# The rare-case test at the end of an attention and mixture-of-experts kernel: where its register is loaded, and where the code it skips lies

## The chip, the cores and the metric

The kernel runs on one core of a Trainium2 chip. The metric is the device time of one execution in microseconds, taken as the median of several runs. Five runs of the kernel before gave a median of 460.94 us, between 460.52 and 461.74. One further execution was taken by the hardware profiler; it took 460.28 us.

## What is computed

Two parts follow each other. The first is multi-query attention: 8 batches of 384 positions, 16 query heads of 64 elements, one key and value head per batch. The second sends each of the 3072 tokens (1024 elements) to one of 16 experts, chosen in two steps, and weighs the expert's answer:

```python
scores = scale * np.matmul(q, k.transpose(0, 1, 3, 2))
attn = np.exp(scores - max) / (sum + 1e-09)
x = np.matmul(attn, v)            # heads side by side: (3072, 1024)
g_idx = argmax(x @ w_group)       # one of 4 groups
e_idx = argmax(xg @ w_expert[g])  # one of 4 experts of the group
h = np.maximum(xg[mask_e] @ w1[g, e], 0.0)
out[tok_idx] = (g_w * e_w)[:, None] * (h @ w2[g, e])
```

## The kernel before, in words

The kernel is built for the case that nearly all tokens of a batch choose the same expert. It runs, for each batch, only the expert that most of its tokens chose, over all 384 tokens of the batch ("first units"). The pairs of batch and expert that this leaves out are counted by flags (`extra`). One such pair, the **leftover**, is picked out with `early_pair` and computed on the main path, for at most 32 tokens. Any more pairs, or scores too large for an exponential without its maximum taken off, are the **rare case**: a block behind `tc.If(rare > 0)` at L809, with loops over the remaining pairs and, inside it, a slow form of the whole computation. With the inputs of this case the block is not entered.

Everything ahead of the block is unrolled, and its order is written out by hand (`tc.manual_schedule()` at L74): each engine runs its instructions in the order in which the source issues them. `fill(n)` puts the next n units of expert work (8 `h_unit`s and 6 `y_unit`s for each batch, L402 and L410) at that place of the order, so that TensorE (PE) has work while small steps wait.

The end of the order is what matters here. Behind the last batch's attention, the flags of the leftover are made (L707: `small`, the number of pairs not covered; L709: `nex`, the same as an integer, on VectorE, DVE). The leftover's tokens are turned (L715, L717), gathered (L723, L725) and sent through its two products: L732 with the Relu at L734 on ScalarE (ACT), a transpose (L738, copied by DVE at L740), and the last product at L746, which ACT scales into `yc` at L748. At L750 GpSimd (POOL) scatters `yc` into the output with an indirect DMA. Between these steps stand single `fill(1)`s. The very last, at L751, is a `y_unit` in two halves: `spread` (L458) first adds the leftover's rows that fall into the last 128 tokens (PE at L463, DVE at L465, ACT at L468, SyncE's (SP) store at L466), then DVE joins each half with `yl` at L454, and SP stores it at L445.

Behind that, from L753 to L758, DVE makes `raref` and `rarei` from `small` and from `okf` (the test of the scores, made at L526), and `nc.values_load` at L758 brings `rarei` into a register on all five engines, with one TENSOR_LOAD on each. L809 is the test of that register. In the built program it is a compare-and-branch on each engine. Which side of it lies next in the code is set by `preferred_fallthrough_block`:

- before, with `False`, the untaken side comes first: a short block on each engine that takes back semaphores (2 semaphore instructions on PE, DVE and ACT each, 9 on SP, 6 instructions on POOL) and ends in a jump over the whole rare block to the kernel's end. The rare block is 836 instructions long in the built program on PE, 212 on DVE, 200 on SP, 145 on POOL and 138 on ACT (PE's fp32 matrix products count once here);
- the kernel's end is the drain and the two barriers over all engines that the profile puts at L901. SP first waits there for the last count of every semaphore (12 instructions), and POOL gathers the five engines.

Of the kernel before, what the change touches and what calls it, by code (L numbers as in the profile page):

```python
# [9 lines left out]
FP32 = mybir.dt.float32  # L10
BF16 = mybir.dt.bfloat16
I32 = mybir.dt.int32
# [3 lines left out]
OP = mybir.AluOpType  # L16
AX = mybir.AxisListType.X
ET = mybir.EngineType
# [3 lines left out]
def kernel(  # L22
# [11 lines left out]
    nc = tc.nc  # L34
# [36 lines left out]
    pool = fast.enter_context(tc.tile_pool(name="work", bufs=2))  # L71
# [4 lines left out]
    def side(shape, dtype, name):  # L76
        return ps_s.tile(shape, dtype, tag="s", name=name)
# [351 lines left out]
    def first_units(b):  # L429
        rows = {}  # L430

        def place(st, cs):
            if cs.start == 0:
                rows[st] = pool.tile([P, Dm], FP32, tag="y", bufs=3, name="y")
            return rows[st][:, cs]

        def closes(st):
            return b == B - 1 and st == ST - 1

        def store(st, cs, y):  # L440
            if closes(st):
                if cs.start == 0:
                    leftover["row"] = y
                else:
                    nc.sync.dma_start(out=outv[b, :, st, cs], in_=y)  # L445
            elif cs.stop == Dm:
                nc.sync.dma_start(out=outv[b, :, st, :], in_=rows[st][:])

        def merge(st, cs, ps, y):
            if not closes(st) or cs.start == 0:  # L450
                return False
            if cs.start == CW:
                spread()
            nc.vector.scalar_tensor_tensor(out=y, in0=ps[:], scalar=gsel[b][:, st:st + 1], in1=leftover["y"][:, cs.start - CW:cs.stop - CW], op0=OP.mult, op1=OP.add)  # L454
            return True
        return moe_units(wts[b][0], wts[b][1], xbf[b], lambda: gsel[b], place, store, merge, lambda st, nh: 2 if closes(st) and nh == 1 else 1)
# [26 lines left out]
    def fill(n):  # L483
        while n > 0:
            if not units:
                if begun[0] >= B or begun[0] not in wts:
                    return
                units.extend(first_units(begun[0]))
                begun[0] += 1
            units.pop(0)()  # L490
            n -= 1
            ran[0] += 1
            if ran[0] == (FO + 2 * ST) * (B - 2) + FO:
                leftover_w1()
            if ran[0] == (FO + 2 * ST) * (B - 1):
                leftover_w2()
# [11 lines left out]
    bound = {}  # L508
# [65 lines left out]
    def leftover_w1():  # L574
        leftover["e"], leftover["b"] = parts_of(leftover["reg"])
        w1 = wpool.tile([P, KO, F], BF16, tag="w1", name="w1")
        load_w1(w1, leftover["e"])
        leftover["w1"] = w1

    def leftover_w2():  # L580
        w2 = wpool.tile([P, FO, Dm], BF16, tag="w2", name="w2")
        nc.gpsimd.dma_start(out=w2[:], in_=w2f[bass.ds(leftover["e"], 1)].rearrange("a p k f -> (a p) k f"))
        leftover["w2"] = w2
# [95 lines left out]
    small = pool.tile([P, 2], FP32, tag="small", bufs=1, name="small")  # L679
# [27 lines left out]
    nc.vector.tensor_sub(out=small[:, 1:2], in0=nfl[:], in1=small[:, 0:1])  # L707
    nex = pool.tile([1, 1], I32, tag="nex", bufs=1, name="nex")
    nc.vector.tensor_copy(out=nex[:], in_=small[0:1, 1:2])  # L709
    fill(3)  # L710
    xtok = []
    for st in range(ST):
# [26 lines left out]
    hc = pool.tile([P, 2, P], BF16, tag="qT", bufs=3, name="hc")  # L739
    nc.vector.tensor_copy(out=hc[:], in_=phT[:])  # L740
    fill(1)
    py = side([P, QW], FP32, "py")
    for g in range(4):
        for h in range(2):
# [2 lines left out]
    yc = pool.tile([P, QW], FP32, tag="pt", bufs=9, name="yc")  # L747
    nc.scalar.activation(out=yc[:], in_=py[:], func=ACTF.Copy, scale=gc[:, 0:1])  # L748
    leftover["yc"] = yc
    nc.gpsimd.indirect_dma_start(out=out4[0:4 * (N - P)], out_offset=bass.IndirectOffsetOnAxis(ap=rows[:], axis=0), in_=yc[:], in_offset=None, bounds_check=4 * (N - P) - 1, oob_is_err=False)  # L750
    fill(1)  # L751
    assert ran[0] == UNITS * B
    raref = pool.tile([1, 2], FP32, tag="raref", bufs=1, name="raref")  # L753
    nc.vector.tensor_scalar(out=raref[:, 0:1], in0=small[0:1, 1:2], scalar1=0.0, scalar2=None, op0=OP.is_gt)
    nc.vector.tensor_scalar(out=raref[:, 1:2], in0=bound["okf"][:], scalar1=-1.0, scalar2=1.0, op0=OP.mult, op1=OP.add)
    rarei = pool.tile([1, 1], I32, tag="rarei", bufs=1, name="rarei")
    nc.vector.tensor_add(out=rarei[:], in0=raref[:, 0:1], in1=raref[:, 1:2])
    rare = nc.values_load(rarei[0:1, 0:1], min_val=0, max_val=2, skip_runtime_bounds_check_because="a sum of two comparisons")  # L758

    def load_pair(pair):  # L760
        e_reg, b_reg = parts_of(pair)
# [44 lines left out]
        for u in pair_units(*load_pair(pair)):  # L806
            u()

    rare_block = tc.If(rare > 0, preferred_fallthrough_block=False)  # L809
    with rare_block:  # L810
      ids = list_rest()
      n_extra = nc.values_load(nex[0:1, 0:1], min_val=0, max_val=NPAIR, skip_runtime_bounds_check_because="a sum of 128 flags")
# [93 lines left out]
```

## Time and profile before

| | us |
|---|---|
| median of the 5 runs | 460.94 |
| the profiled execution | 460.28 |
| its span, first to last instruction | 458.8 |
| PE busy | 448.7 |
| DVE busy | 308.4 |
| ACT busy | 242.0 |
| POOL busy | 60.5 |

The profiled execution's own time holds 1.5 us that lie outside its span. All durations below come from that execution, and times of day count from the span's start. In the profile, an engine's name with a q behind it (SPq, PEldq) stands for its sequencer: register loads, branches, semaphore instructions and the issue of DMAs, which are not counted as busy time. PE's sequencer goes under PEldq, since PEld is its weight load. A line such as "L758 SPq TENSOR_LOAD x1: 551/551/551, 453.4 to 453.4" gives the shortest, median and longest duration in ns, and the first and the last start in us. Instructions themselves are fetched by DMA: the page lists 35 pieces (0.57 MB) on queue 8 and 19 (0.16 MB) on queue 14 for the whole span.

### The profile page before, as it was taken

Reading aid. Unit: us, or ns where it says so; the run is one execution under the profiler, and the core shown is the slowest. Engines: PE = TensorE matmul, PEld = TensorE weight load, DVE = VectorE, ACT = ScalarE, POOL = GpSimd, SP = SyncE. Lnnn points to the kernel's source line nnn. Section 1 sums busy time; section 2 is a strip of 40 time slices with the busy share of each in tenths; the row PEclk is TensorE's granted clock in tenths of the full one; section 3 lists DMA queues with packets and bytes.
Section 4 is the critical chain, followed back from the end, with each engine's and each line's share of the span. In section 5 each row is a group of like instructions: output and inputs, shape, how many; then the busy total and the mean of one; then the engine's idle time right before and its main releaser. Section 6 shows DMA issues by size and latency. Waiting matters only on the chain.

```text
span 458.8 us, 10188 instructions
## 1 busy us (share of the span) xinstructions
PE 448.7 (98%) x4196; PEld 199.8 (44%) x4208; DVE 308.4 (67%) x488; ACT 242.0 (53%) x345; POOL 60.5 (13%) x83
## 2 busy tenths in 40 slices
PE   8999999999999999999999999999999999999994
PEld 6333445333643345433553335433364334434552
DVE  4899965499717996099843997269970999573421
ACT  2966643676337753566346663376635764541331
POOL 1004003000120113000030000300130000500000
PEclk9999999999999999999999999999999999999998
DMA  8787997996699395992979848994859910799992
GB/s 161 92 147 113 216 215 112 259 201 138 108 181 255 71 196 88 233 228 72 156 110 261 152 108 134 160 258 89 170 97 231 235 59 28 110 210 233 277 230 105
DMA packets 152454, 74.55 MB, mean 162 GB/s; under 512 B 120256, under 2 KB 138944, under 8 KB 152400
## 3 DMA queue, kind: packets, MB, share of 16 engines
q0 software_dynamic: 28416, 37.81, 48.3%
q1 hardware_dynamic: 122656, 35.68, 33.4%
q8 instruction: 35, 0.57, 0.5%
q10 hardware_dynamic: 1328, 0.33, 0.3%
q14 instruction: 19, 0.16, 0.1%
HBM read 92.62 MB, written 19.01 MB: 243 GB/s over the span
## 4 chain that ended last, share of the span: by engine, by line
PE 89%; DMA 4%; issue 3%; DVE 1%; POOL 0%; ACT 0%; ACTq 0%; SPq 0%; POOLq 0%
PE s L251 28%; PE o L290 25%; PE hps L407 17%; PE yps L417 16%; PE gps L312 2%; DMA x_bf<-xbf 2%; DMA xe<-x_bf 2%; DMA qn<-in_q_dram 1%; PE qps L228 1%; POOL xbf L301 0%; DVE presum L261 0%; PE sm L273 0%; PE pb L715 0%; DVE rinv L280 0%; DVE xT L300 0%
## 5 line engine op out<-in xcount | busy, mean ns | idle before, releaser
L253 ACT ACTIVATE pt<-s 128x1024 f32<-128x1024 f32 x144 | 142.1, 1026 | 72.2 <-PE s L251 71.5
L251 PE MATMUL s<-qT,kT 64*64 64x512 f32 x1152 | 142.7, 594 | 0.0
L290 PE MATMUL o<-pt,v 64*64 64x512 f32 x1152 | 141.1, 590 | 0.0
L261 DVE TENSOR_TENSOR presum<-presum,pt 128x1024 f32<-128x1024 f32 x96 | 116.6, 1215 | 15.2 <-ACT pt L253 9.8
L407 PE MATMUL hps<-xbf,w 128*128 128x384 bf16 x512 | 86.7, 326 | 0.0
L417 PE MATMUL yps<-w,hT 128*128 128x512 bf16 (+1 forms) x380 | 85.0, 375 | 0.6
L259 DVE TENSOR_TENSOR presum<-pt 128x1024 f32<-128x1024 f32 x24 | 29.4, 1224 | 76.8 <-ACT pt L253 75.4
L290 PEld LDWEIGHTS o<-pt,v 64*64 64x64 f32 x1152 | 43.4, 133 | 76.8 <-issue 73.0
L251 PEld LDWEIGHTS s<-qT,kT 64*64 64x64 f32 x1152 | 40.8, 133 | 66.8 <-issue 60.0
L301 POOL CAST xbf<-xT 128x1024 bf16<-128x1024 f32 x24 | 25.0, 1043 | 302.7 <-DVE xT L300 302.7
L407 PEld LDWEIGHTS <-w 128*128 128x128 bf16 x512 | 48.2, 98 | 37.6 <-issue 6.5
L419 ACT ACTIVATE y<-yps,gsel 128x512 f32<-128x512 f32 x47 | 32.3, 687 | 58.8 <-PE yps L417 57.2
L408 ACT ACTIVATE hT<-hps 128x384 bf16<-128x384 f32 x64 | 31.3, 489 | 51.9 <-PE hps L407 47.8
L417 PEld LDWEIGHTS <-hT 128*128 128x128 bf16 x392 | 37.6, 98 | 44.1 <-issue 2.4
L145 POOL DMA_DIRECT2D w<-in_moe_w_dram x36 | 24.8, 708 | 58.1 <-DVE gsel L395 37.6
L300 DVE TENSOR_TENSOR xT<-o,rinv 128x1024 f32<-128x1024 f32 x24 | 29.2, 1215 | 2.5 <-PE o L290 2.5
L280 DVE STREAM_TRANSPOSE rinv<-rc 128x1024 f32<-128x1024 f32 x24 | 29.9, 1246 | 0.8
L265 DVE TRANSPOSE_TENSOR_REDUCE fold<-presum 128x32 f32<-128x1024 f32 x24 | 29.6, 1232 | 0.0
L243 DVE STREAM_TRANSPOSE qT<-qraw 128x1024 f32<-128x1024 f32 x20 | 23.6, 1203 | 0.0
L209 ACT ACTIVATE qraw<-qraw 128x1024 f32<-128x1024 f32 x21 | 22.0, 1048 | 0.0
L273 PEld LDWEIGHTS sm<-fold,sel 64*64 64x64 f32 x192 | 7.3, 133 | 13.3 <-issue 13.3
L371 ACT ACTIVATE ex<-dl 128x60 f32<-128x60 f32 x8 | 2.0, 253 | 20.1 <-DVE dl L369 20.1
(152 smaller groups left out, 161.9 us busy)
## 6 DMA issues: line engine op xcount, KB each, us to landing
w<-in_moe_w_dram POOLq DMA_DIRECT2D x36, 512.0 KB, 11.6
w<-in_moe_w_dram POOLq DMA_DIRECT2D x9, 2048.0 KB, 25.9
out_dram<-y SPq DMA_DIRECT2D x23, 512.0 KB, 7.1
qraw<-in_q_dram SPq DMA_DIRECT2D x56, 192.0 KB, 3.7
x_bf<-xbf SPq DMA_DIRECT2D x8, 768.0 KB, 3.9
v<-in_v_dram SPq DMA_DIRECT2D x16, 96.0 KB, 3.4
k<-in_k_dram SPq DMA_DIRECT2D x28, 48.0 KB, 3.0
qn<-in_q_dram SPq DMA_DIRECT2D x4, 256.0 KB, 5.2
```

The source lines that it names most:

```text
L251: nc.tensor.matmul(out=ps[64 * c:64 * c + 64, a, :], lhsT=kT[b][r, j * D:(j + 1) * D], rhs=qT[p][r, c * CW:(c + 1) * CW], start=True, stop ...
L253: nc.scalar.activation(out=t[:], in_=ps[:], func=ACTF.Exp, scale=scale)
L259: nc.vector.tensor_add(out=presum[p][:], in0=pt[p, 0][:], in1=pt[p, 1][:])
L261: nc.vector.tensor_add(out=presum[p][:], in0=presum[p][:], in1=pt[p, j][:])
L265: nc.vector.tensor_reduce(out=fold[p][:], in_=presum[p][:].rearrange("p a (n i) -> p (a n) i", i=32), axis=AX, op=OP.add, apply_transpose= ...
L280: nc.vector.transpose(out=t[:].rearrange("p (b i) -> p b i", i=32), in_=rc[:].rearrange("p c b -> p (c b)").unsqueeze(2).to_broadcast([P, ...
L290: nc.tensor.matmul(out=o_ps[p][64 * a:64 * a + 64, c, :], lhsT=v_sb[b][r, j, :], rhs=pt[p, j][r, a, :], start=(j == 0), stop=(j == KB - 1))
L300: nc.vector.tensor_mul(out=xT[b][:, :, ts], in0=o_ps[p][:].rearrange("p c (h n) -> p (c h) n", n=P), in1=rinv[p][:].rearrange("p (h n) -> ...
L407: nc.tensor.matmul(out=ps[:, 0:S], lhsT=w1[:, ko, fc * P:(fc + 1) * P], rhs=xb[:, ko, :], start=(ko == 0), stop=(ko == KO - 1))
L408: nc.scalar.activation(out=state["h"][:, fc, :], in_=ps[:, 0:S], func=ACTF.Relu)
L417: nc.tensor.matmul(out=ps[:], lhsT=state["h"][:, fo, st * P:(st + 1) * P], rhs=w2[:, fo, cs], start=(fo == 0), stop=(fo == FO - 1))
L419: nc.scalar.activation(out=y, in_=ps[:], func=ACTF.Copy, scale=gs_of()[:, st:st + 1])
```

## The change

Four edits belong together. The three DVE instructions that make `raref` and `rarei` move from behind the last unit to behind `nex`. The load of the register, on all five engines, moves from behind the last unit to just ahead of the leftover's last product. The untaken side of the test is no longer the one that follows it in the code: it now lies behind the rare block, next to the kernel's end. And a prefetch hint for the test's branch, "likely taken", is put on PE alone, behind the leftover's last product and its `yc`, with a barrier for the scheduler alone (no instruction) ahead of it.

```diff
     nc.vector.tensor_copy(out=nex[:], in_=small[0:1, 1:2])
+    raref = pool.tile([1, 2], FP32, tag="raref", bufs=1, name="raref")
+    nc.vector.tensor_scalar(out=raref[:, 0:1], in0=small[0:1, 1:2], scalar1=0.0, scalar2=None, op0=OP.is_gt)
+    nc.vector.tensor_scalar(out=raref[:, 1:2], in0=bound["okf"][:], scalar1=-1.0, scalar2=1.0, op0=OP.mult, op1=OP.add)
+    rarei = pool.tile([1, 1], I32, tag="rarei", bufs=1, name="rarei")
+    nc.vector.tensor_add(out=rarei[:], in0=raref[:, 0:1], in1=raref[:, 1:2])
     fill(3)
...
     nc.vector.tensor_copy(out=hc[:], in_=phT[:])
     fill(1)
+    rare = nc.values_load(rarei[0:1, 0:1], min_val=0, max_val=2, skip_runtime_bounds_check_because="a sum of two comparisons")
     py = side([P, QW], FP32, "py")
...
     leftover["yc"] = yc
+    tc.no_sync_barrier()
+    tc.mark_branch_hint_location("rare", hint="LikelyTaken", engines=(ET.PE,))
     nc.gpsimd.indirect_dma_start(out=out4[0:4 * (N - P)], ...)
     fill(1)
     assert ran[0] == UNITS * B
-    raref = pool.tile([1, 2], FP32, tag="raref", bufs=1, name="raref")
-    nc.vector.tensor_scalar(out=raref[:, 0:1], in0=small[0:1, 1:2], scalar1=0.0, scalar2=None, op0=OP.is_gt)
-    nc.vector.tensor_scalar(out=raref[:, 1:2], in0=bound["okf"][:], scalar1=-1.0, scalar2=1.0, op0=OP.mult, op1=OP.add)
-    rarei = pool.tile([1, 1], I32, tag="rarei", bufs=1, name="rarei")
-    nc.vector.tensor_add(out=rarei[:], in0=raref[:, 0:1], in1=raref[:, 1:2])
-    rare = nc.values_load(rarei[0:1, 0:1], min_val=0, max_val=2, skip_runtime_bounds_check_because="a sum of two comparisons")
...
-    rare_block = tc.If(rare > 0, preferred_fallthrough_block=False)
+    rare_block = tc.If(rare > 0, preferred_fallthrough_block=True, label="rare")
```

In the built program the TENSOR_LOADs stand behind PE's weight load of the first product of L746, ahead of `yc` on ACT, behind the copy `hc` on DVE, ahead of the store of L466 on SP, and ahead of the indirect DMA on POOL. PE's hint stands behind the last product of L746.

## The prediction

> **What bounds the kernel now.** I read the page first.
>
> ```profile
> span 458.8 us, 10188 instructions
> ...
> PE 448.7 (98%) x4196; PEld 199.8 (44%) x4208; DVE 308.4 (67%) x488; ACT 242.0 (53%) x345; POOL 60.5 (13%) x83
> ```
>
> TensorE bounds the kernel as a whole, but no work of TensorE is removed, so the share of 98% does not price this change. What counts is what stands behind the last product. The timeline of the end shows it:
>
> ```profile
> 451.47 1.09 POOL L750 DMA_INDIRECT out_dram<-yc,rows  x1 [25.62 <-issue]
> 451.64 0.88 DVE L454 SCALAR_TENSOR_TENSOR y<-yps,gsel,yl 128x256 f32<-128x256 f32 x2
> ...
> 452.50 0.83 SPq L445 DMA_DIRECT2D out_dram<-y  x2
> 452.66 0.15 DVE L757 TENSOR_TENSOR rarei<-raref 1x1 int32<-1x1 f32 x1
> ```
>
> The last counted instruction ends at 452.8, and the span at 458.8: 6.0 us in which no engine computes. The queries for lines L758, L810 and L901 show what fills them (op and count, shortest/median/longest ns, first and last start):
>
> ```profile
> L758 PEldq TENSOR_LOAD <-rarei x1: 648/648/648, 452.8 to 452.8; - x1
> L758 SPq TENSOR_LOAD <-rarei x1: 551/551/551, 453.4 to 453.4; - x1
> ```
>
> ```profile
> L810 ACTq COMPARE_BRANCH  x2: 38/44/49, 453.5 to 453.8; - x2
> L810 POOLq COMPARE_BRANCH  x2: 38/41/44, 453.5 to 455.4; - x2
> L810 DVEq COMPARE_BRANCH  x2: 51/53/55, 453.6 to 453.9; - x2
> L810 PEldq COMPARE_BRANCH  x2: 95/1933/3771, 453.6 to 454.0; - x2
> ...
> L810 SPq COMPARE_BRANCH  x2: 38/46/53, 454.0 to 455.5; - x2
> ```
>
> ```profile
> L901 SPq EVENT_SEMAPHORE  x14: 17/28/28, 456.0 to 458.7; - x14
> ...
> L901 POOLq DRAIN  x3: 46/103/871, 455.8 to 458.5; - x3
> L901 SPq DRAIN  x3: 7/7/13, 456.7 to 458.2; - x3
> L901 ACTq DRAIN  x2: 8/44/80, 456.7 to 458.2; - x2
> L901 DVEq DRAIN  x2: 10/34/57, 456.9 to 458.2; - x2
> L901 PEldq DRAIN  x2: 8/40/73, 457.9 to 458.3; - x2
> ```
>
> Each engine tests the register at 453.5 to 454.0 and then jumps over the rare block. PE's jump alone has a duration of 3771 ns, and PE reaches the end's first drain last of all, at 457.9. ACT and DVE jump too: ACT at 453.8, arriving at 456.7, and DVE at 453.9, arriving at 456.9, about 3.0 us each. POOL and SP arrive 0.45 us after theirs (455.4 to 455.8, 455.5 to 456.0). The view of DMAs between 454.1 and 457.9 has seven instruction fetches, among them one piece of 16 KB on queue 8, the larger kind. I read the long jumps as code that has to be fetched, the short ones as code that was there already. The waits of SP say who was late:
>
> ```profile
> SPq L901 <- PEq L901: 1.9, 2, 1.4
> ```
>
> So the tail is: DVE's flags, register load, test, PE's jump, and then 0.9 us of barriers (457.9 to 458.8).
>
> **The change, part by part.**
>
> *Flags.* Three DVE instructions (130, 131 and 148 ns) move from 452.4 to about 431.1, behind L709. DVE then idles 4.6 us until 435.72 (L717 waits for PE), which hides them; without that cover they would cost 0.4 us.
>
> *Register load.* 0.55 to 0.65 us leave the end on every engine, and the branch no longer waits for DVE. At the new place each load must hide. On DVE it follows `hc` and lies in the 4.1 us idle before L465; on SP in the 4.2 us wait before L466; on POOL in the 25.6 us before L750; `rarei` is then long written. On ACT it stands between L419 (448.40 to 449.09) and `yc` (449.35). The semaphore instruction of L748 already runs at 448.4, beside L419, so the load runs from about 448.45 to 449.10 and leaves 0.25 us. Where DVE loaded a register at 394.9 for 545 ns, its next TENSOR_SCALAR started at 395.04, inside it: such a load does not wait for the engine. If it did here, `yc` would start at 449.74, and 0.4 us would be passed on to everything behind. On PE the load stands ahead of the products of L746, which start at 448.24; their operand `hc` is ready at 446.91. The load would end by 447.6, 0.6 us before PE's array comes free of L417. That its sequencer runs ahead is seen in L746's semaphore instruction, at 445.8. I take 0; from both sides this cost is 0 to 0.65 us.
>
> *Hint.* No row shows such an instruction. By the nearest rows, PE's semaphore instruction of 51 ns and the register load of 648 ns, it costs 0.05 to 0.65 us of sequencer time, ahead of weight loads that themselves follow a 0.2 us gap; I take 0, by the nearer row.
>
> *Layout.* The same two branches run on each engine. The long jump is now the test itself, and the short one, from the untaken side into the end, follows it. The rare block is as long as before, so I take the fetch classes as before: long on PE, ACT and DVE, short on POOL and SP. What differs is when the jump is made, since it waits for nothing on DVE or in memory. Arrivals at L901, each taken late:
>
> - PE: last product over at 451.9. Without any help from the hint, 451.9 + 3.8 = 455.7, two semaphore instructions and a branch 0.4 (453.6 to 454.05), short jump 0.45: 456.6. With the hint, sent at about 449.0 behind L746, the fetch is over at 452.8 and PE arrives at 453.7.
> - ACT: L468 over at 451.6, + 3.0 + 0.3 + 0.45 = 455.4.
> - DVE: L454 over at 452.5, + 3.0 + 0.3 + 0.45 = 456.3.
> - POOL: the indirect DMA issued at 451.5 lands 3.2 us later, at 454.7. Its semaphores wait for that and not for the branch; from there as now: branch 455.4, drain at 455.8 for 871 ns, 456.7.
> - SP: the last store, issued at 452.9, lands 2.3 us later, at 455.2; from there as now: branch 455.5, twelve waits from 456.0, drains over at 456.8.
>
> The next late thing is thus a pair, POOL's drain and SP's waits, at 456.7 to 456.8 where PE stood at 457.9 with 0.07 of drain: the gain is **1.1 to 1.2 us**. The hint gives nothing of it by this sum; the earlier branch gives it all, because PE's fetch then runs beside the landing of the last stores.
>
> One row may give a little more. SP's wait of L445 starts at 452.4, 0.35 us behind the end of L466's issue (451.75 + 0.33), where 0.04 is usual (L447: 442.08 + 0.33, next at 442.46), and a fetch on queue 14 starts 1.1 us later, at 453.5. If that is the border of a code block, the load now placed ahead of L466 moves it into idle time and SP comes at 456.4. POOL keeps the end at 456.7, so this is worth 0.1 us.
>
> [...]
>
> **Rivals.**
>
> 1. *The covers are too short.* ACT's load delays `yc` by 0.4 us, or PE's load or hint delays L746, or SP's jump, now made at 453.4, meets a block still in flight. That last is priced by the fetch seen at 453.5 and the 1.4 us that ACT's fetch needed after its transfer: usable at 455.3, then nine semaphores 0.7, jump 0.45, twelve waits 0.8, 457.3. Each leaves 0.4 to 0.8 us of the gain: about 460.3. For it speak the 0.25 us on ACT; against it the slack elsewhere.
> 2. *The stall stays on the path.* The change does not do what it says: PE's sequencer reaches the branch only when the last stores do, by a wait that I don't see. Then 3.8 us stand behind 454.0 as now: 460.9, no change. Against it: the untaken side on PE waits for PE's own counts alone.
> 3. *Two fetches instead of one: slower.* If a code block's border falls between the untaken side and the end, on PE or DVE, an engine fetches at the test and again at the short jump. On DVE 456.3 - 0.45 + 3.0 = 458.9, on PE 456.6 - 0.45 + 3.8 = 459.9 without the hint, against 457.9 now: 1.0 to 2.0 us slower, 462 to 463. It decides as soon as the second fetch starts after about 455. For it: nothing in the source places the blocks. Against it: the side is only 3 instructions long on these engines.
>
> **How the numbers follow.** The profiled execution took 460.28, 1.5 us more than its span; the sum makes the span 457.6 and this execution 459.1. The median of five runs lies 0.66 above the profiled execution, so I forecast 460.94 - 1.2 = **459.7**, its own range 459.3 to 460.0. Chances: forecast 0.62, rival 1 0.22, rival 2 0.07, rival 3 0.09. With rival 1 and its full bound (a gain of 0.4) the range is 459.3 to 460.6, which leaves out rivals 2 and 3. A measurement of this kernel tells about 0.2% (0.92 us) from no change; the forecast's gain, 0.26%, is just beyond that. Faster: 0.62 × 0.95 and a sixth of rival 1, 0.62. Slower: 0.09. The rest, 0.29, is the same.
>
> **What would show it.** In the profile after, PE's drain at L901 stands before POOL's and SP's, and SP no longer waits there for PE. The test on PE runs at about 452, ACT's and DVE's before 453. The last store of L445 is issued at 452.5 to 452.9 as now, and `yc` starts at 449.35: if either is later, a load or the hint was not hidden. POOL's long drain still starts at 455.8, and from the last drain to the end 0.9 us pass. With a working hint, a fetch on queue 8 starts at about 450 and PE's branch is short; without one it stays near 3.8 us, harmlessly. I am wrong if PE or DVE still arrives last, or if POOL's and SP's 456.7 hangs on the branch rather than on the landings.

## The result and the profile after

The changed kernel takes 459.65 us in the median (26 runs, 459.31 to 462.27), the kernel before 461.0 us in the 49 runs beside them. The ratio is 0.9979, with a 95% interval of 0.9972 to 0.9985: a gain of about 1 us, small, but with an interval that leaves out 1. Four of the 26 runs lie at 461.6 to 462.3; none of them was traced, and why is open (of the 42 runs of e1, e2, e8, e9 and e10 below, which end much like it, none lies above 460.7). The medians, which these four hardly move, differ by 1.35 us; the means, of which they raise the one, by 1.0 us. The profiled execution took 459.4 us.

```profile
span 457.9 us, 10184 instructions
...
PE 448.7 (98%) x4196; PEld 199.8 (44%) x4208; DVE 308.3 (67%) x488; ACT 241.9 (53%) x345; POOL 60.4 (13%) x83
```

No work was removed: busy times are those of before. Lines have moved: the register load is L747, the leftover's last product `py` L752, the indirect DMA L758, the test L812, the end L903. The query for L812 answers to that for L810 of before:

```profile
L812 PEldq EVENT_SEMAPHORE  x2: 51/51/51, 454.5 to 454.7; - x2
...
L812 PEldq COMPARE_BRANCH  x1: 3956/3956/3956, 450.5 to 450.5; - x1
L812 ACTq COMPARE_BRANCH  x1: 50/50/50, 451.3 to 451.3; - x1
...
L812 DVEq COMPARE_BRANCH  x1: 72/72/72, 452.2 to 452.2; - x1
L812 SPq COMPARE_BRANCH  x1: 50/50/50, 453.9 to 453.9; - x1
```

Two things are to be seen. PE's test now stands at 450.5 in place of 453.6 and carries the long fetch itself. And each engine has one branch where it had two: the untaken side runs on into the end, and the short jump, which cost POOL and SP 0.45 us before, is gone. The query for the end, L903:

```profile
L903 POOLq DRAIN  x3: 46/103/802, 456.1 to 457.6; - x3
L903 SPq DRAIN  x3: 7/7/13, 457.0 to 457.3; - x3
L903 ACTq DRAIN  x2: 8/8/8, 454.1 to 457.3; - x2
L903 PEldq DRAIN  x2: 7/8/8, 454.8 to 457.4; - x2
L903 DVEq DRAIN  x2: 10/14/17, 456.0 to 457.4; - x2
```

PE drains at 454.8, long before SP at 457.0; before, it came last, at 457.9. SP's waits, in the window from 444 to 459, say the same. The 1.9 us for PE have fallen to the barriers' own 0.7, and SP now waits in its untaken side:

```profile
SPq L812 <- SPq L812: 1.9, 4, 0.8
SPq L903 <- PEq L903: 0.7, 2, 0.5
```

What SP waits for there is shown by the view of DMAs from 450 us to the end. Its last lines give, for each issue, the median us to landing. The kernel before:

```profile
out_dram<-y SPq DMA_DIRECT2D x1, 256.0 KB, 2.3
out_dram<-y SPq DMA_DIRECT2D x2, 128.0 KB, 2.3
out_dram<-yc,rows POOLq DMA_INDIRECT x1, 3.2
```

and after:

```profile
out_dram<-y SPq DMA_DIRECT2D x1, 256.0 KB, 2.8
out_dram<-y SPq DMA_DIRECT2D x2, 128.0 KB, 2.9
out_dram<-yc,rows POOLq DMA_INDIRECT x1, 3.4
```

The same stores of the same size (L466 in the first line, the two of L445 in the second) take 0.5 to 0.6 us longer to land. The rows of L445 show that one of its issues lasts longer too, first before, then after:

```profile
L445 SPq DMA_DIRECT2D out_dram<-y x2: 336/386/436, 452.5 to 452.9; - x2
```

```profile
L445 SPq DMA_DIRECT2D out_dram<-y x2: 417/652/887, 452.5 to 453.4; - x2
```

Neither was in the forecast, and the experiments follow them.

**One clock for all runs.** The profiled executions reach the product `py` between 448.2 and 449.6 us, and why they differ there was not looked into. From here on times count from the first weight load of `py` ("at 5.4"), and the tail is the time from there to the end of the span: 10.54 us before, 9.39 after. Fetches are pieces on queue 8 (16 KB each) and queue 14 (8 KB each), with their start from the trace's DMA records. I take those on queue 8 for PE's, since PE's long jump ends 1.4 to 1.6 us behind the end of one (before, after, e2, e3, e4), and those on queue 14 for the other engines'; no view names the engine.

### The profile page after: what moved, and what is told of

The parts are those of the page before. It is cut to its first block, busy times and chain, and to the rows that moved or that the text cites. A ratio compares the mean times of both kernels' runs of the same rounds, so it can differ in the third digit from the quotient of the medians.

```text
span 457.9 us, 10184 instructions
## 1 busy us (share of the span) xinstructions
PE 448.7 (98%) x4196; PEld 199.8 (44%) x4208; DVE 308.3 (67%) x488; ACT 241.9 (53%) x345; POOL 60.4 (13%) x83
## 4 chain that ended last, share of the span: by engine, by line
PE 91%; DMA 3%; issue 3%; DVE 1%; POOL 1%; ACT 0%; SPq 0%; POOLq 0%; ACTq 0%
PE s L251 28%; PE o L290 25%; PE hps L407 17%; PE yps L417 16%; PE gps L312 2%; DMA x_bf<-xbf 2%; DMA xe<-x_bf 2%; PE qps L228 1%; PE warm L152 1%; POOL xbf L301 0%; DVE presum L261 0%; PE sm L273 0%; PE pb L720 0%; DVE rinv L280 0%; DVE xT L300 0%
```

## The experiments

The theories: **A**, the forecast's: branching earlier gives the gain, because PE's fetch then runs beside the landing of the last stores. **B**: the hint gives it. **C**: the layout gives it. **D**: the fetches delay the issue and the landing of the last stores, so that part of the gain is given back. **E**: the scatter or the stores themselves came nearer to the end.

| kernel | median us | ratio to before, 95% | PE drains at | PE's fetches start at | L445's stores land at | tail us |
|---|---|---|---|---|---|---|
| before | 461.0 | 1 | 9.64 | -1.24, 6.71, 10.24 | 6.64, 6.94 | 10.54 |
| after | 459.65 | 0.9979 (0.9972 to 0.9985) | 6.30 | 1.79, 2.96, 7.12 | 7.11, 7.48 | 9.39 |
| e1 after again | 459.79 | 0.9972 (0.9963 to 0.9982) | 6.28 | 1.79, 2.95, 6.58 | 7.08, 7.39 | 9.30 |
| e2 no hint | 459.58 | 0.9975 (0.9966 to 0.9985) | 6.32 | 1.79, 3.49, 6.82 | 7.09, 7.41 | 9.32 |
| e3 early load only | 461.17 | 1.0007 (0.9998 to 1.0016) | 8.09 | 1.79, 5.17, 8.65 | 7.73, 8.14 | 10.80 |
| e4 layout only | 461.46 | 1.0010 (1.0001 to 1.0019) | 10.03 | -0.34, 6.30, 10.34 | 6.72, 7.51 | 11.19 |
| e5 no rare block | 459.77 | 0.9963 (0.9949 to 0.9976) | 1.99 | 0.95 | 6.23, 7.05 | 9.09 |
| e6 early hint, all engines | 460.92 | 0.9996 (0.9987 to 1.0005) | 4.47 | 1.77, 5.41 | 7.88, 8.21 | 10.38 |
| e7 early hint, PE | 460.59 | 0.9991 (0.9982 to 1.0000) | 4.47 | 1.77, 5.41 | 7.76, 8.09 | 10.25 |
| e8 earlier load, hint | 459.58 | 0.9965 (0.9951 to 0.9979) | 4.00 | -1.51, 3.15 | 7.10, 7.48 | 9.39 |
| e9 earlier load, no hint | 459.87 | 0.9973 (0.9963 to 0.9983) | 6.12 | -0.94, 2.92, 6.44 | 7.14, 7.42 | 9.34 |
| e10 as e8, control | 459.63 | 0.9971 (0.9961 to 0.9982) | 4.00 | -1.32, 3.69 | 7.10, 7.41 | 9.32 |
| e11 8 idle products | 460.65 | 0.9993 (0.9984 to 1.0002) | 5.73 | -1.46, 4.59 | 8.48, 8.72 | 10.63 |
| e12 14 idle products | 461.05 | 1.0001 (0.9992 to 1.0010) | 7.02 | -1.05, 5.31 | 8.17, 8.50 | 10.66 |

### e1 and e2: once more, and without the hint

e1 is the changed kernel, unaltered. e2:

```diff
-    tc.no_sync_barrier()
-    tc.mark_branch_hint_location("rare", hint="LikelyTaken", engines=(ET.PE,))
```

> The changed kernel, unaltered, beside the others of this call. Theory A (the early branch lets PE's 3.9 us code fetch run beside the landing of the last stores; the end is then SP's and POOL's wait for those landings): 459.4 to 459.9, SP the last engine to reach the final barrier, PE there some 2 us earlier. Theory B (the hint on PE does it) and theory C (the moved block does it) expect the same time here. What is open: in the first profile the second issue of the last stores took 887 ns where the kernel before had 336 ns, and the stores landed about 0.5 us later; if that is a cost of the fetches that now run beside the stores, it shows again; if it was chance, the issues are near 0.34 and 0.44 us.

> The changed kernel without the prefetch hint on PE. Theory A: no loss, within 0.2 us of the changed kernel (459.4 to 459.9), PE's test still near 3.9 us long and PE still early at the final barrier (before 455.5). Theory B: the gain is lost wholly or in good part, 460.4 or more, with PE late. Theory C: no loss.

Measured: the two are alike, 0.9972 and 0.9975, and PE's test lasts 3936 ns with the hint and 3972 ns without. The change's hint does nothing; theory B falls. The slow issue shows again: the first store of L445 is issued in 889 and 919 ns, so it was not chance.

### e3 and e4: each half alone

e3 keeps the early flags and the early load, without the hint and with the old layout; e4 is the kernel before with the new layout alone.

```diff
# e3, from after
-    rare_block = tc.If(rare > 0, preferred_fallthrough_block=True, label="rare")
+    rare_block = tc.If(rare > 0, preferred_fallthrough_block=False)
# e4, from before
-    rare_block = tc.If(rare > 0, preferred_fallthrough_block=False)
+    rare_block = tc.If(rare > 0, preferred_fallthrough_block=True)
```

> Only the flags and the register load are early; the untaken side stands behind the test as in the kernel before, and there is no hint. Theory A: most of the gain stays. PE takes the long jump out of the untaken side at about 452.3 and reaches the end at about 456.2; POOL and SP make their short jump of 0.45 us behind the landings, which the changed kernel does not have, so about 0.4 us slower than the changed kernel: 459.9 to 460.3. Theory B and theory C: the gain is gone, 460.8 to 461.1.

> Only the untaken side is moved next to the kernel's end; flags and register load stay behind the last unit, no hint. Theory A: PE's long jump is now the test itself, at 453.6 instead of 454.05, and the two semaphore instructions come behind it, so PE still arrives last, at about 457.8: 460.7 to 461.0, a gain of at most 0.2 us. Theory C: the gain is here, 459.4 to 460.0. Theory B: no gain.

Measured: **neither gains anything**, 1.0007 and 1.0010. Theories A and C, each taken alone, fall. e3's queries for L812 and, below it, L903 show that PE is no longer late, and that the time is not won all the same:

```profile
L812 PEldq COMPARE_BRANCH  x2: 95/2040/3984, 450.5 to 452.5; - x2
```

```profile
L903 SPq DRAIN  x3: 7/7/13, 458.2 to 458.8; - x3
...
L903 PEldq DRAIN  x2: 8/17/26, 456.6 to 458.8; - x2
```

PE drains 1.6 us ahead of SP. But in the old layout the long jump stands behind the untaken side, which first waits for PE's products: the test is made at 1.99, the semaphores come at 3.71, the jump at 4.00, and its fetch starts at 5.17 in place of 2.96. That is when the last stores move their data (355 GB/s at that time). e3's view of DMAs from 450 us on:

```profile
out_dram<-y SPq DMA_DIRECT2D x1, 256.0 KB, 2.6
out_dram<-y SPq DMA_DIRECT2D x2, 128.0 KB, 3.8
out_dram<-yc,rows POOLq DMA_INDIRECT x1, 4.5
```

3.8 us where before has 2.3, and SP still pays its short jump behind it (8.42 to 8.91). Against e2, which differs from e3 by the layout alone, SP drains 1.24 us later (9.67 for 8.43): 0.73 us of that is the last landing, and the rest is mostly the jump. POOL waits for its scatter, which lands 1.1 us later than in e2, and ends 0.2 us behind SP. In e4 the load stays late, PE's test at 5.34 waits 4336 ns for its code, and PE still ends the kernel (query for L901):

```profile
L901 SPq DRAIN  x3: 7/7/13, 459.4 to 459.7; - x3
...
L901 PEldq DRAIN  x2: 8/8/8, 459.2 to 459.8; - x2
```

SP's 459.4 follows PE's 459.2 here: the trace has it wait 1.2 us for PE's L810 in its row of twelve. So the two edits are worth something only together.

### e5: no far jump

The whole rare block and its test are left out (with them the register load falls away), and the hint too, so this kernel computes only the case of these inputs.

```diff
-    rare_block = tc.If(rare > 0, preferred_fallthrough_block=True, label="rare")
-    with rare_block:
-      ...
```

> The changed kernel without the hint and with the whole rare block and its test left out (the branch that these inputs never take); flags and register load stay. No engine jumps far, so no code is fetched beside the last stores. Theory D (the fetches that the early jumps start delay the issue and the landing of the last stores; with the gain of the early branch and this loss the changed kernel comes out at 0.9 to 1.3 us): the two stores of L445 are issued in about 0.34 and 0.44 us, they land 2.3 us after their issue as in the kernel before, SP passes its waits for them at 6.4 and 6.7 us behind the first product of L752 (7.1 and 7.4 to 7.5 with the block), and the time falls by a further 0.8 to 1.0 us, to 458.6 to 459.0. Rival E (the slow issue and landing come from the indirect scatter, or from the stores following each other closer): they stay at 0.9 us and 7.4, and the time falls by less than 0.4.

Measured: 459.77 in five runs, one of them at 458.72, ratio 0.9963; not below after by anything that can be told. The view of DMAs from 451 us on says that with one 8 KB piece (at 5.79) left of the fetches the stores of L445 land as quickly as before:

```profile
q14 instruction: 1, 0.01, 0.2%
...
out_dram<-y SPq DMA_DIRECT2D x1, 256.0 KB, 2.1
out_dram<-y SPq DMA_DIRECT2D x2, 128.0 KB, 2.3
```

But another transfer was late. The store of L447, issued at -1.02, had 15 of its 16 landings by 1.58 and the last at 3.96, with a fetch of PE from 0.95 to 1.91 beside it; the scatter started only behind that, at 5.11 in place of 3.45, and landed at 7.52; SP waits 2.4 us for it at the end. So the tail fell by 0.30 us and not by the 0.8 to 1.0 expected. In that execution `py` also started 0.5 us later than in after (449.03 for 448.51), for a reason that was not looked into. e5 does not test theory E by itself, since its scatter moved out of the stores' way. e12 below does: there the scatter starts at 3.35 and the first store of L445 is issued at 3.94, as in after (3.45 and 3.94), and the issue takes 378 ns in place of 887. So the spacing of the scatter and the stores does not by itself make the issue slow; for the landing theory E stays untested.

### e6 and e7: the hint some 7 us earlier

The hint moves from behind `yc` to ahead of the product `ph` (L737), on all five engines in e6, on PE alone in e7.

```diff
+    tc.no_sync_barrier()
+    tc.mark_branch_hint_location("rare", hint="LikelyTaken", engines=(ET.PE,))
     ph = side([P, QW], FP32, "ph")
...
-    tc.no_sync_barrier()
-    tc.mark_branch_hint_location("rare", hint="LikelyTaken", engines=(ET.PE,))
```

> The changed kernel with the hint on all five engines, ahead of the leftover's first product (L737), about 7 us before the branches instead of 2 on PE alone. If a hint fetches the named code: PE's test falls from 3.9 us to under 0.5, ACT's and DVE's gaps behind their tests from 2.7 and 3.5 us to about 0.5, the fetches lie ahead of the last stores and by theory D these land 0.5 to 0.8 us earlier: 458.9 to 459.3. If a hint does nothing that lasts until the branch (as the hint of the changed kernel seemed to): 459.5 to 459.9, tests as long as before. If hints displace the code that comes next: slower, 460 or more.

> The same early hint, on PE alone. If hints work with this lead: PE's test under 0.5 us, its fetch gone from the 2.9 us mark; the last stores land up to 0.3 us earlier (ACT's and DVE's fetches stay): 459.2 to 459.7. If not: as the changed kernel, 459.5 to 459.9, test 3.9 us.

Measured: placed so early, the hint works on PE: the test lasts 2126 ns in place of 3956, and PE drains at 4.47 in place of 6.30. **And the kernel becomes slower than after**, 460.92 (e6) and 460.59 (e7). For e7 none of the named cases had that; for e6 the third had the time, with a cause (other code displaced) that nothing here shows. PE has two fetches where it had three, and the second starts at 5.41 where after has none between 2.96 and 7.12; the stores of L445 land 3.8 to 3.9 us after their issue. On ACT and DVE the hint does not shorten the jump (in e6 their untaken sides start at 5.28 and 7.85, in after at 5.44 and 7.24).

### e8 and e9: the register load earlier too

```diff
     w1c, w2c = leftover["w1"], leftover["w2"]
+    rare = nc.values_load(rarei[0:1, 0:1], ...)
+    tc.no_sync_barrier()                                                          # e8 only
+    tc.mark_branch_hint_location("rare", hint="LikelyTaken", engines=(ET.PE,))    # e8 only
     ph = side([P, QW], FP32, "ph")
...
-    rare = nc.values_load(rarei[0:1, 0:1], ...)
     py = side([P, QW], FP32, "py")
...
-    tc.no_sync_barrier()
-    tc.mark_branch_hint_location("rare", hint="LikelyTaken", engines=(ET.PE,))
```

> The register load moves ahead of the product into `ph` (L737), on all five engines, and PE's hint stands right behind it. Times are counted from the first weight load of the product into `py`. Theory D (the kernel's time goes by where PE's code fetches fall beside the data of the last stores): PE's fetch of the next block, which started at 1.8 with the load just ahead of this product, starts near -1.2 as in the kernel before, the hint of some 6 us earlier makes it fetch the branch's target, PE's test is shorter than 0.5 us, and PE's next fetch falls ahead of the stores' issue at 3.9; the stores of L445 then land at 7.1 or earlier and the kernel takes 458.9 to 459.6. If instead the next fetch falls between 5 and 6.5, theory D says that the stores land at 7.7 or later and the kernel takes 460.3 to 461.0. Theory A (the earlier branch alone decides): not above 459.65 in either case.

> The same earlier register load, without a hint. Theory D: PE's test lasts about 4 us as in the changed kernel; its time goes by the landing of the stores of L445, 459.4 to 459.9 if they land at 7.1 to 7.5, about 460.3 or more if a fetch of PE falls at 5 to 6.5 and they land at 7.7 or later. Theory A: as the changed kernel, 459.4 to 459.9, wherever the fetches fall.

Measured: e8's test on PE lasts 397 ns, e9's 3766 ns. The queries for L812, first e9, then e8:

```profile
L812 PEldq COMPARE_BRANCH  x1: 3766/3766/3766, 450.8 to 450.8; - x1
```

```profile
L812 PEldq COMPARE_BRANCH  x1: 397/397/397, 451.2 to 451.2; - x1
```

PE drains at 4.00 in e8, 2.3 us earlier than after, and this is worth nothing: 459.58 against 459.65, with tails of 9.39 both. (The time is one that theories A and D both allowed; of D's stores only the first landed at 7.1, the second at 7.48.) e8's PE fetches at 3.15, ahead of the stores' data, and nothing later. Beside e6, which moves the same packets, the one large difference is when that one fetch on queue 8 runs (queue 14 has six pieces in each, at times up to 0.6 us apart). The view of DMAs from 451 to 459, first e6 (fetch at 5.41), then e8 (fetch at 3.15):

```profile
DMA packets 487, 0.65 MB, mean 81 GB/s; under 512 B 80, under 2 KB 336, under 8 KB 480
...
q8 instruction: 1, 0.02, 0.9%
...
out_dram<-y SPq DMA_DIRECT2D x2, 128.0 KB, 3.9
out_dram<-yc,rows POOLq DMA_INDIRECT x1, 4.5
```

```profile
DMA packets 487, 0.65 MB, mean 81 GB/s; under 512 B 80, under 2 KB 336, under 8 KB 480
...
q8 instruction: 1, 0.02, 1.1%
...
out_dram<-y SPq DMA_DIRECT2D x2, 128.0 KB, 2.9
out_dram<-yc,rows POOLq DMA_INDIRECT x1, 3.6
```

### e10 to e12: moving the fetch by work that nobody waits for

e10 is e8 unaltered. To e11 and e12, 8 and 14 products are added behind the last unit and ahead of the test, into a tile that nobody reads.

```diff
-    fill(1)
+    fill(1); idle = side([P, CW], FP32, "idle"); [nc.tensor.matmul(out=idle[:], lhsT=ones_bf[:], rhs=w2c[:, 0, 0:CW], start=True, stop=True) for _ in range(8)]   # 14 in e12
```

> The kernel with the earlier load and hint once more, unaltered, as the control of the two kernels with idle products. All theories: 459.4 to 459.9, PE's test 0.4 us, PE's next fetch 3.1 us behind the product into `py`, the stores of L445 landing 2.9 us after their issue.

> To the control are added 8 products of TensorE into a tile that nobody reads, behind the last unit and ahead of the test: 8 x 0.27 = 2.1 us of PE's time that no engine waits for; the output stays the reference's. PE is ready at about 6.1 behind the product into `py` in place of 4.0, still ahead of SP and POOL at 8.4. Theory D (fetches beside the stores' data make them land late): PE's fetch moves from 3.1 to about 5.2, the stores of L445 land 3.8 us after issue and the kernel takes 460.1 to 460.8. Theory A (only who arrives last counts): as the control, 459.4 to 459.9.

> The same with 14 idle products, 3.8 us. PE is ready at about 7.8, still ahead of SP and POOL at 8.4; its fetch starts at about 6.9, when 13 of 16 parts of each store of L445 have landed. Theory D: stores land at most 3.0 us after issue, 459.2 to 459.9, faster than with 8 products although PE has more to do. A theory by which late work on PE itself costs the time: slower than with 8 products, 460.5 or more. Theory A: as the control.

Measured: 459.63, 460.65 and 461.05. The idle products cost 1.0 and 1.4 us, although PE is ready in both cases well ahead of SP. The query for L903 in e11:

```profile
L903 SPq DRAIN  x3: 7/7/13, 459.4 to 459.7; - x3
...
L903 PEldq DRAIN  x2: 8/8/8, 455.3 to 459.7; - x2
```

In e11 PE stands 4.1 us ahead of SP and still sets the time, by when its fetch runs: 4.59 in e11, 5.31 in e12, 3.69 in the control. e11's view of DMAs from 451 us on (the control's second line has 2.7 us):

```profile
out_dram<-y SPq DMA_DIRECT2D x1, 256.0 KB, 4.5
out_dram<-y SPq DMA_DIRECT2D x2, 128.0 KB, 4.4
out_dram<-yc,rows POOLq DMA_INDIRECT x1, 5.0
```

e12's expectation failed: I had its fetch at 6.9, behind the data, and wanted it faster than e11. PE's sequencer makes the test at 3.49 whether 8 (3.43) or 14 products stand before it, and the fetch came at 5.31; why that is 0.7 us behind e11's is open. The stores were as late as a fetch at that time makes them elsewhere (e3, e6, e7). The fetch behind the data was thus not tried by this means; before itself has one, at 6.71, and its stores land after 2.3 us. What came in is the time that I had named for the rival, late work on PE itself (slower than with 8 products, 460.5 or more), though the tails of the two are alike, 10.63 and 10.66. Against that rival: e3, e6 and e7 have no such work, and their stores are late too.

The landings show how. A store is recorded as 16 landings. In e12, 15 of the 16 of L466's store have landed by 6.11, of the scatter by 7.07, of L445's two stores by 6.85 and 7.38; the last one of each comes at 7.84, 8.34, 8.17 and 8.50. One sixteenth of each of these four is late, by 1.1 to 1.7 us, and these last parts follow each other by 0.16 to 0.33 us. (In e3, e6 and e7 it is three or four parts of the last store.) The DMA records of the trace show what this sixteenth waited for. L466's store is 128 packets of 2 KB. In e12, 120 of them have started by 5.29; the other eight start one behind the other from 6.32, as PE's fetch ends (6.34), and eight packets of each store of L445 follow them. In e11 120 have started by 5.25, and the other eight start from 6.37, with the fetch's end at 6.39. So in these two runs one sixteenth of the store starts only as the fetch ends. Why it is this sixteenth is open; the trace does not name the DMA engine of a piece.

The issue of a store is held up as well. In seven runs (after, e1, e2 and e8 to e11) PE's fetch is under way when SP begins to issue a store of L445, or starts 0.2 us later (e11). In all seven that issue ends 0.37 to 0.42 us behind the fetch's end, however long that makes it: 0.67 us in e9, 0.89 in after, 2.38 in e11, whose last store is late as a whole for this. The other issues of L445 take 0.34 to 0.52 us, save for the second one in e3, e6 and e7 (0.63 to 0.92 us), which ends 0.13 us behind a piece on queue 14. L466's issue keeps its 0.34 us even beside a fetch of PE, so what holds the one and not the other is open.

## Why the prediction was right, and where it was not

The time and its sign were right (459.7 against 459.65), and so was who comes last: SP and POOL, with PE off the end. The way there was right in part, and the sum came out by luck as well.

- **Flags and loads at no cost: right.** ACT's load took 753 ns and ended 0.18 us ahead of `yc`; PE's took 488 ns at 447.2. `yc` starts 1.11 us and `lo` 1.97 us behind `py` in both kernels, so rival 1's covers were long enough.
- **The hint gives nothing: right for this place,** by e2: PE's test takes 3956 ns in after, with the hint, and 3972 ns without. A hint 4.5 us ahead of PE's next fetch did act: it cut the test from 3766 to 397 ns (e9 and e8).
- **"The earlier branch gives it all": this step failed.** With the early load alone nothing was gained (e3). The layout was in my sum only as the order of two jumps. What it does is to let the test jump at once, at 1.99, while the old untaken side first waits for PE's last product; only so does the fetch come ahead of the stores' data (it starts at 3.49 in e2 and at 5.17 in e3; in after the first packet of L466's store starts at 4.35, of L445's at 5.36). In my sum the new test, too, came behind the last product, at about 452; it ran at 450.5.
- **"The same two branches run on each engine": wrong.** The second is gone, which takes 0.45 us off SP and POOL.
- **"The last store lands 2.3 us later": wrong, 2.6 us in after,** and its issue was late too. The late issue comes from PE's fetch, by the seven runs above. For the 0.3 us of the landing the cause is open: the last store took 2.55 us in e8 and 2.27 in e10, both with a fetch of PE just ahead of it, as in after, and 2.37 in e5 with none. I suspect the pieces on queue 14 (in after five start between 3.72 and 6.44, in the kernel before one up to that time, at 5.27); no run removed those alone.
- **SP's gap: gone, as forecast.** The gap behind L466's issue fell from 0.35 to 0.05 us in every kernel with the early load, and in e5, where a semaphore instruction stands in the load's place; it stayed in e4. That a code border was its cause was not tested.

The sizes of the missing jump and of the late last store cancel, which is luck, and this is why the sum came out. My sum had SP drain at 8.56. By the trace its last store was issued 0.23 us later than I took it (4.89 for 4.66, since the issue before it took 887 ns), and took 0.3 us longer to land; from there to the drain it took 1.02 us for my 1.6, 0.45 of which is the missing jump. It drained at 8.50. Where they did not cancel the same working failed: its forecast for e3, 459.9 to 460.3, was 0.9 to 1.3 us too low.

What rival 2 priced (the stall stays at the end) is seen in e4, there by the late load: PE at 10.03, behind everything. Rival 3 (two fetches in a row) was not seen: in after PE fetches again at 7.12, but it had reached the end by then.

## What to carry to other kernels

In these runs an engine that nobody waited for still set the end, by when its instruction fetches fell: taking 2.3 us off PE's arrival was worth nothing (e8), and moving its fetch by 0.9 us with idle work cost 1 us (e11). So when a branch or a code layout is moved near the end of a kernel, look first for when the fetches start and which transfers are under way then, and only after that for who arrives last. Two edits that do nothing alone (e3, e4) can be worth their whole gain together; try the halves before crediting one.

## What the runs showed of the hardware

- **From jump to code on PE.** Where PE's jump was long and no hint acted, a piece of 16 KB on queue 8 started 0.9 to 1.5 us behind the jump (before 6.71 for 5.80, after 2.96 for 1.99, e2 3.49 for 1.99, e3 5.17 for 4.00), took 0.9 to 1.5 us, and PE's next instruction ran 1.4 to 1.6 us after its end: 3.8 to 4.0 us together, and 4.3 in e4, where the transfer took 1978 ns.
- **A hint shortened the test in some places and not in others.** Where it stood 4.5 us (e8) or 8.5 us (e7) ahead of the start of PE's next fetch, PE's test took 397 ns (3766 without, e9) and 2126 ns; at 1.65 us (after) it took 3956 ns, and 3972 without (e2). What lies between was not tried.
- **Late stores beside a fetch.** With a fetch of PE started between 4.6 and 5.4 (e3, e6, e7, e11, e12), L445's second store, issued at 4.4, was complete 3.7 to 4.3 us later; with one started up to 3.7 or from 6.3 on, 2.3 to 2.9 us after its issue. In e11 and e12 the last eight of the 128 packets of L466's store started as the fetch ended (6.37 for 6.39, 6.32 for 6.34).
- **A late issue beside a fetch.** Where PE's fetch met the start of an issue of L445 on SP, the issue ended 0.37 to 0.42 us behind the fetch's end (after, e1, e2, e8 to e11); L466's, beside the same fetch, kept its 0.34 us.
- **The time of a register load varied.** 298 to 488 ns on PE, DVE and SP in after, where they stand apart, against 551 to 648 ns before on PE and SP, where all five engines loaded within 0.6 us; but 753 ns on ACT in after, alone. So company is not the whole reason, and what is was not tested.
